# Transposing attention scores by half rows of TensorE, two at a time, in an attention and two-layer MLP kernel

## The chip, the core and the metric

The kernel runs on one core of one Trainium2 chip. The core has TensorE for matmuls (PE in the profile; its weight loads are listed apart as PEld), VectorE (DVE), ScalarE (ACT), GpSimd (POOL) and SyncE (SP), which issues most of the DMAs. The metric is the time of one execution on the device in microseconds (us), the median of a few runs.

## What is computed

Three stages follow one another. All arrays are float32.

```python
batch, n_heads, seq, head_dim = (2, 12, 448, 64)
scores = np.matmul(q, k.transpose(0, 1, 3, 2)) / np.sqrt(64)   # causal mask above the diagonal
attn = np.exp(scores - max) / (sum + 1e-9)
out = np.matmul(attn, v)                       # heads side by side: x, 896 tokens x 768
h = x @ w_in;  g = h * np.clip(h + 3, 0, 6) / 6;  x = g @ w_out     # 768 -> 2048 -> 768
h = x @ w_in2; g = P(h) / (Q(h) + 1e-6);          y = g @ w_out2    # P cubic, Q in |h| and h*h
```

## The kernel before

**Attention.** The heads are worked on two at a time: 12 pairs, each of one batch and two heads. The 448 query rows of a head are cut into seven strips of 64 rows, r = 0 to 6, and strip r looks at (r + 1) * 64 keys. The strip r of both heads lies in one tile of 128 partitions, one head on each half; these are the tiles e_91 to e_97 (r = 0 to 6) for even pairs and e_98 to e_104 for odd pairs. The steps of a pair n are:

- `scores`: 14 matmuls, each on a quarter of TensorE (64 rows by 64 columns), into four PSUM banks;
- `max` on DVE, seven instructions: masked scores go to the e tiles, with the maximum of each row (the profile's CUSTOM_DVE_ANT_0, L457, and a short read of the accumulator);
- `exp` on ACT, seven, each with the sum of its rows; `bias` and `reciprocal` of the sums, once for the strips 6, 5, 0 ("straight") and once for 4, 3, 2, 1 ("swapped");
- `norm`: the e tiles times the reciprocals, on POOL (L488) for the pairs 1 to 9, and on POOL, DVE or ACT for the others;
- `transpose` (L494): the e tiles are cut into 16 blocks of 128 rows by 128 keys, in four groups (`GROUPS`) of four, each group into one bank;
- `move` (L497 f., a copy on DVE or ACT): one bank of 512 columns to SBUF, four times a pair;
- `apply` (L514): 16 matmuls of the transposed blocks with v, on the two column halves of TensorE, into one bank o;
- `x hi` on ACT and `x rest` on DVE (L526, writes xl): o is split into two float32r parts.

**Products.** Each matrix product is made of three TensorE passes of 448 columns (high by high, low by high, high by low parts; xh, xl and so on in the profile). Weights come in chunks of three tiles. A chunk goes through `w load` (a DMA into raw), `top` (ACT), `join` (DVE, L641, writes full), `w hi` (ACT or POOL) and `w rest` (DVE or POOL, L659). All 2304 matmuls of the products stand at L729. The sums of the products may hold all eight PSUM banks, and no product may start before the last pair's scores (`scored`).

**What sets the order.** Nothing is written down in program order. `Program.order` is a list scheduler that runs when the kernel is built: each step has a cost for each engine that may do it, a due time (the pair's own time `t`, 5.5 apart, plus `DUE` of its kind and, for some pairs, `SHIFT`), and the tiles that it reads, writes and allocates. It picks the step that can begin first (within `LOOK`) and, among equals, that which is due first; `STAY` is added to the due time of a step that would put TensorE into another tiling (`TILING`). `banks` limits how many PSUM banks each use holds: scores 4, transposes 2 ("t"), o 1, out of eight. On the chip each engine then works through its own queue in that order, waiting on semaphores.

Of the kernel before, what the change touches and what calls it, by code (L numbers as in the profile page):

```python
# [8 lines left out]
F32 = mybir.dt.float32  # L9
# [10 lines left out]
P = 128  # L20
CP = 64
# [19 lines left out]
class Program:  # L41
# [13 lines left out]
    }  # L55
    BANKS = 8

    TILING = {"scores": "quarters", "apply": "columns"}
    DRAIN = 0.16
    STAY = 22.65  # L60
    LOOK = {"pe": 0.244, "dve": 0.000, "act": 0.000, "pool": 0.830, "dma": 0.000}
    UNTIL = 90.0

    def __init__(self, rings, banks, due):
# [3 lines left out]
    def add(self, kind, at, engines, fn, *args, reads=(), writes=(), new=()):  # L68

        self.ops.append((kind, at, engines, fn, args, tuple(reads), tuple(writes), tuple(new)))
# [124 lines left out]
def c_act(n):  # L197
    return 0.051 + n / 1200


def c_dve(n):
    return 0.068 + n / 960
# [12 lines left out]
def c_pe(n, passes):  # L215
    return passes * (0.0025 + n / 2400)
# [6 lines left out]
def c_mm(n, passes):  # L223
# [2 lines left out]


DUE = {
    "load": -169.78,
    "keep": 0.00,  # L230
    "fetch": -20.00,
    "load v": -160.42,
    "norm": -298.28,
    "scores": 315.32,
    "max": 50.63,
    "exp": 213.93,
    "bias": -18.96,
    "reciprocal": 22.57,
    "transpose": -74.01,
    "move": 210.62,  # L240
    "apply": -55.68,
    "x hi": 156.92,
    "x rest": 260.06,
    "constants": 64.75,
    "w load": -41.79,
    "top": 181.03,
    "join": 339.16,
    "w hi": 262.44,
    "w rest": 56.54,
    "product": 0.00,  # L250
    "relu": -117.34,
    "gate": 172.42,
    "g hi": -99.35,
    "g rest": 280.77,
    "y hi": 20.80,
    "y rest": 12.60,
    "affine": 7.80,
# [13 lines left out]
    "store": 7.50,  # L271
}
PAIR = 5.5
SHIFT = {0: -20.39, 1: -6.41, 2: -0.83, 10: 17.95, 11: 31.46}


def plan(KM, KF):
# [17 lines left out]
def tile_attention_moe_moe2(  # L295
# [24 lines left out]
    def skew(pool, size):  # L320
# [7 lines left out]
    EB, VB = 2, 3  # L328
    rings = {
        "raw": 5, "full": 3, "top": TOPS, "w": 4,  # L330
        "qr": 4, "kr": 4, "v": 3, "stat": 3, "et": 6,
        "p": 4, "qy": 3,
    }
    rings.update({f"e{r}": EB for r in range(NCH)})
    prog = Program(rings, {"s": 4, "t": 2, "o": 1, "sum": 8}, DUE)
    add = prog.add
    bank = [psum.tile([P, 512], F32, name=f"bank{n}") for n in range(prog.BANKS)]

# [3 lines left out]
    def copy(e, out, in_):  # L342
        if e is nc.scalar:
            e.activation(out, in_, AF.Copy)  # L344
        else:
            e.tensor_copy(out, in_)


    def x_tiles(nm):
# [8 lines left out]
    at = attn.enter_context(tc.tile_pool(name="at", bufs=2))  # L358
    tiles = {}

    ident = at.tile([P, P], F32, name="ident", bufs=1)
# [4 lines left out]
    halves = [slice(j * D, (j + 1) * D) for j in range(2)]  # L366
    blocks = [r // 2 + 1 for r in range(NCH)]
    es = [
        [at.tile([P, P * blocks[r]], F32, name=f"e{r}{x}", bufs=1) for r in range(NCH)]
        for x in range(EB)  # L370
    ]
    vs = [at.tile([P, KB, 2 * D], F32, name=f"v{x}", bufs=1) for x in range(VB)]
# [26 lines left out]
    for x in range(EB):  # L399
# [3 lines left out]
        new=[("o", "warm")],  # L403
# [10 lines left out]
    def v_load(e, n):  # L414
# [7 lines left out]
    SCORES = 0, 2, 6, 4, 5, 1, 3  # L422
    BANKS = ((6, 0), (4, 2), (5,), (3, 1))
    GROUPS = [
# [4 lines left out]
    ]  # L429
    APPLY = [[0, 1, 2, 3]]  # L430

    def slots(r):
        return (0, 1) if r in STRAIGHT else (1, 0)
# [54 lines left out]
            e.tensor_scalar(t, t, by, 1.0, ALU.mult, ALU.mult)  # L488

    def a_transpose(e, n, g, banks):  # L490
        pt = tiles["pt", n, g] = bank[banks[0]]
        to = pt.rearrange("p (s b q) -> p b s q", s=2, q=CP)
        for x, (r, c) in enumerate(GROUPS[g]):
            e.transpose(to[:, x], es[n % EB][r][:, c * P:(c + 1) * P], ident)  # L494

    def a_move(e, n, g):
        et = tiles["et", n, g] = at.tile([P, 512], F32, tag="et", name=f"et{n}_{g}", bufs=rings["et"])  # L497
        copy(e, et, tiles.pop(("pt", n, g)))

    def a_apply(e, n, a, banks=None):  # L500
        if a == 0:
            tiles["o", n] = bank[banks[0]]
        o, vt = tiles["o", n], vs[n % VB]
        for g in APPLY[a]:
            et = tiles.pop(("et", n, g)).rearrange("p (s b q) -> p s (b q)", s=2, q=CP)
            runs = []
            for x, (r, c) in enumerate(GROUPS[g]):
                if runs and runs[-1][2] == c and runs[-1][1] + runs[-1][3] == r:
                    runs[-1][3] += 1
                else:  # L510
                    runs.append([x, r, c, 1])
            for m, (x, r, c, count) in enumerate(runs):
                for j, slot in enumerate(slots(r)):
                    e.matmul(  # L514
                        o[halves[j], r * CP:(r + count) * CP], vt[:, c, halves[j]],
                        et[:, slot, x * CP:(x + count) * CP], start=g == 0 and m == 0,
                        stop=g == len(GROUPS) - 1 and m == len(runs) - 1,
                    )

# [11 lines left out]
    for n in range(len(pairs)):  # L531
        t, last = PAIR * n + SHIFT.get(n, 0.0), n == len(pairs) - 1
        for which in ("kr", "qr"):
            raw = which, n
            add(
                "load", t, {"act" if n == 0 and which == "qr" else "dma": 1.26}, qk_load, which, n,
                writes=[raw], new=[(which, raw)],
            )
        add(
            "load v", t, {"dma": 0.9}, v_load, n, reads=[("empty", n % VB)], writes=[("v", n), ("turn", "v")],  # L540
            new=[("v", ("v", n))],
        )
        sc = [("sc", n, held) for held in BANKS]
        add(
            "scores", t, {"pe": 1.42}, a_scores, n, reads=[("kr", n), ("qr", n)],
            writes=sc + ["scored"] * last, new=[("s", key) for key in sc],
        )
        for late, r in enumerate(order):
            w, first, mine = (r + 1) * CP, late == 0, next(held for held in BANKS if r in held)
            add(  # L550
                "max", t + late, {"dve": c_dve(w)}, a_max, n, r,
                reads=[("sc", n, mine), "masks"] + [("stat", n)] * (not first)
                + [("m", n, mine[0])] * (r != mine[0]),
                writes=[("e", n, r), ("st", n, r), ("m", n, r), ("turn", r)] + [("stat", n)] * first,
                new=[(f"e{r}", ("e", n, r))] + [("stat", ("stat", n))] * first,
            )
            add(
                "exp", t + late, {"act": 0.235 + c_act(w)}, a_exp, n, r, reads=[("stat", n)],
                writes=[("e", n, r), ("st", n, r)],
            )  # L560
        for part, held in enumerate((STRAIGHT, SWAPPED)):
            add(
                "bias", t + 2 * part, {"act": 0.2, "dve": 0.1}, a_bias, n, part,
                reads=[("st", n, r) for r in held] + [("stat", n)], writes=[("r", n, part)],
            )
            add(
                "reciprocal", t + 2 * part, {"dve": 0.15}, a_recip, n, part, reads=[("stat", n)],
                writes=[("r", n, part)],
            )
            for r in held:  # L570
                w = (r + 1) * CP
                add(
                    "norm", t + 2 * part, c_norm(n, r, w), a_norm, n, r,
                    reads=[("r", n, part), ("stat", n)], writes=[("e", n, r)],
                )
        for g, group in enumerate(GROUPS):
            add(
                "transpose", t + g, {"pe": 0.436}, a_transpose, n, g,
                reads=["masks", ("pads", n % EB)] + [("e", n, r) for r in sorted({r for r, _ in group})],
                writes=[("pt", n, g)], new=[("t", ("pt", n, g))],  # L580
            )
            add(
                "move", t + g, {"act": c_act(512), "dve": c_dve(512)}, a_move, n, g,
                reads=[("pt", n, g)], writes=[("et", n, g)], new=[("et", ("et", n, g))],
            )
        for a, gs_ in enumerate(APPLY):
            cols = 1024 * len(gs_) // len(GROUPS)
            add(
                "apply", t + 2 * a, {"pe": c_pe(cols, 4) + 0.08}, a_apply, n, a,
                reads=[("et", n, g) for g in gs_] + [("v", n)], writes=[("o", n)],  # L590
                new=[("o", ("o", n))] if a == 0 else (),
            )
        b, hp = pairs[n]
        add("x hi", t, {"act": c_act(S)}, a_hi, n, reads=[("o", n)], writes=[("x", hp, b)])
        add("x rest", t, {"dve": c_dve(S)}, a_lo, n, reads=[("o", n)], writes=[("x", hp, b)])
# [372 lines left out]
```

## Time and profile before

| | before |
|---|---|
| median of 3 runs | 547.02 us (546.81 to 547.05) |
| the profiled execution | 547.23 us |
| its span, first to last instruction | 545.4 us |
| PE busy | 535.4 us (98%) |
| PEld busy | 491.7 us (90%) |
| DVE busy | 363.0 us (67%) |
| ACT busy | 342.5 us (63%) |
| POOL busy | 37.5 us (7%) |

The first matmul begins 2.07 us into the span; attention takes the first 82 us, products the rest. PE's busy time is the union of its instructions, whose ends are modelled, so being busy does not mean that the array streams at its peak.

### The profile page before, as it was taken

To read this page: it belongs to the slowest core of one execution; us is meant where nothing else is said; L and a number is where in the kernel's file an instruction comes from. 1 tells how busy PE (TensorE), PEld (TensorE's weight loads), DVE (VectorE), ACT (ScalarE), POOL (GpSimd) and SP (SyncE) were. 2 spreads that over 40 slices of the span, in tenths; PEclk is the share of its full clock that TensorE was granted. 3 is DMA by queue.
4 is the path that set the end of the run, shared out by engine and by line. 5 is a ranking of instruction groups with operands and counts; after the bars stand their busy time and mean duration, and the time that the engine had idled before them with its cause. 6 is when DMAs were issued, how large, how long until landed. Compare 5 with 4: busy or idle time off the path is not lost.

```text
span 545.4 us, 9102 instructions
## 1 busy us (share of the span) xinstructions
PE 535.4 (98%) x3236; PEld 491.7 (90%) x3236; DVE 363.0 (67%) x814; ACT 342.5 (63%) x752; POOL 37.5 (7%) x91
## 2 busy tenths in 40 slices
PE   6999999999999999999999999999999999999997
PEld 5778889999999999999999998899999999999996
DVE  3789975677877765445543189988888888853310
ACT  4899985576777665455443187776777677645210
POOL 2486500000000000000000000000000000000000
PEclk9899999999999999999999999999999999999999
DMA  6787402477877778767775321543343234236100
GB/s 165 200 250 207 139 2 88 136 240 219 268 232 264 236 248 269 269 218 241 234 282 157 107 87 59 165 124 88 96 134 119 87 100 133 88 118 205 46 34 34
DMA packets 39309, 87.07 MB, mean 160 GB/s; under 512 B 4704, under 2 KB 14688, under 8 KB 39264
## 3 DMA queue, kind: packets, MB, share of 16 engines
q1 hardware_dynamic: 39104, 86.27, 50.2%
q8 instruction: 25, 0.41, 0.3%
q10 hardware_dynamic: 160, 0.23, 0.1%
q14 instruction: 20, 0.16, 0.1%
HBM read 71.14 MB, written 15.34 MB: 159 GB/s over the span
## 4 chain that ended last, share of the span: by engine, by line
PE 92%; DVE 5%; ACT 1%; DMA 1%; issue 0%; POOL 0%; POOLq 0%; ACTq 0%; DVEq 0%
PE bank L729 79%; PE bank L494 4%; PE bank L514 4%; PE bank L445 4%; PE bank L394 1%; DVE e L457 1%; DMA w<-kept 1%; DVE qy L794 1%; DVE p L778 1%; DVE p L804 1%; DVE p L781 0%; DVE qy L802 0%; DVE rl L788 0%; DVE p L806 0%; ACT p L774 0%
## 5 line engine op out<-in xcount | busy, mean ns | idle before, releaser
L729 PE MATMUL bank<-yh,w 128*128 128x448 f32 x384 | 112.0, 362 | 1.2 <-DVE w L659 1.2
L636 ACT ACTIVATE top<-raw 128x384 f16<-128x384 bf16 x128 | 78.7, 639 | 46.1 <-DVE full L641 39.6
L659 DVE TENSOR_TENSOR w<-full,w 128x384 fp32r<-128x384 f32 x94 | 52.5, 558 | 77.0 <-ACT w L344 76.9
L344 ACT ACTIVATE w<-full 128x384 fp32r<-128x384 f32 x92 | 48.3, 525 | 82.8 <-PE bank L729 82.7
L729 PE MATMUL bank<-rh,w 128*128 128x448 f32 x384 | 97.3, 363 | 0.4 <-DMA w<-kept 0.4
L729 PE MATMUL bank<-xh,w 128*128 128x448 f32 x384 | 93.4, 363 | 0.0
L729 PE MATMUL bank<-ph,w 128*128 128x448 f32 x384 | 92.5, 362 | 0.0
L729 PEld LDWEIGHTS bank<-yh,w 128*128 128x128 f32 x384 | 71.9, 187 | 6.2 <-DVE w L659 1.6
L729 PEld LDWEIGHTS bank<-rh,w 128*128 128x128 f32 x384 | 71.8, 188 | 5.9 <-ACT qy L797 0.8
L729 PEld LDWEIGHTS bank<-ph,w 128*128 128x128 f32 x384 | 72.0, 188 | 5.0
L729 PEld LDWEIGHTS bank<-xh,w 128*128 128x128 f32 x384 | 71.7, 188 | 5.0
L641 DVE SCALAR_TENSOR_TENSOR full<-raw,top 128x384 uint32<-128x384 uint32 x128 | 69.1, 558 | 1.5
L729 PE MATMUL bank<-yl,w 128*128 128x448 f32 x192 | 69.6, 363 | 0.0
L729 PE MATMUL bank<-rl,w 128*128 128x448 f32 x192 | 54.3, 361 | 0.0
L729 PE MATMUL bank<-pl,w 128*128 128x448 f32 x192 | 53.9, 362 | 0.0
L729 PE MATMUL bank<-xl,w 128*128 128x448 f32 x192 | 53.9, 362 | 0.0
L464 ACT ACTIVATE e<-e,stat 128x448 f32<-128x448 f32 (+6 forms) x84 | 42.5, 526 | 8.0 <-DVE stat L457 8.0
L729 PEld LDWEIGHTS bank<-yl,w 128*128 128x128 f32 x192 | 36.0, 188 | 2.6
L729 PEld LDWEIGHTS bank<-rl,w 128*128 128x128 f32 x192 | 36.0, 187 | 2.5
L457 DVE CUSTOM_DVE_ANT_0 e<-bank,mask 128x256 f32<-128x256 f32 (+6 forms) x84 | 31.6, 414 | 9.9 <-PE bank L445 9.8
L729 PEld LDWEIGHTS bank<-pl,w 128*128 128x128 f32 x192 | 36.0, 187 | 2.2
L729 PEld LDWEIGHTS bank<-xl,w 128*128 128x128 f32 x192 | 36.0, 187 | 2.2
(59 smaller groups left out, 646.9 us busy)
## 6 DMA issues: line engine op xcount, KB each, us to landing
raw<-in_w SPq DMA_DIRECT2D x128, 383.8 KB, 3.6
kept<-ws SPq DMA_DIRECT2D x32, 384.0 KB, 4.6
w<-kept SPq DMA_DIRECT2D x32, 384.0 KB, 3.3
kr<-in_kT SPq DMA_DIRECT2D x24, 112.0 KB, 3.6
out_T<-o SPq DMA_DIRECT2D x12, 224.0 KB, 2.8
qr<-in_qT SPq DMA_DIRECT2D x22, 112.0 KB, 3.3
v<-in_v SPq DMA_DIRECT2D x12, 128.0 KB, 3.1
v<-in_v SPq DMA_DIRECT2D x12, 96.0 KB, 3.5
```

The lines of the kernel that those rows point to most:

```text
L344: e.activation(out, in_, AF.Copy)
L394: e.matmul(bank[banks[0]][:, :P], ident, ident, start=True, stop=True)
L445: e.matmul(tiles["sc", n, r][halves[slot]], q[halves[j], r * CP:w], k[halves[j], :w], start=True, stop=True,)
L457: e.tensor_tensor_reduce(es[n % EB][r][:, :w], tiles.pop(("sc", n, r)), mask[:, S - w:], -0.125, 3.0e38, ALU.add, ALU.min, tiles["stat", n ...
L464: e.activation(t, t, AF.Exp, bias=stat[:, 0, at_:at_ + 1], scale=-1.0, accum_out=stat[:, 1, at_:at_ + 1],)
L494: e.transpose(to[:, x], es[n % EB][r][:, c * P:(c + 1) * P], ident)
L514: e.matmul(o[halves[j], r * CP:(r + count) * CP], vt[:, c, halves[j]], et[:, slot, x * CP:(x + count) * CP], start=g == 0 and m == 0, stop ...
L636: e.activation(out, raw[i].bitcast(BF16)[:, :, :, 2], AF.Copy)
L641: e.scalar_tensor_tensor(full[i].bitcast(U32), bits, 13, top.pop(i), ALU.logical_shift_right, ALU.bitwise_or)
L659: e.tensor_tensor(split[i][:, 1], full.pop(i), split[i][:, 0], ALU.subtract)
L729: e.matmul(sums[which, m, b], split[i][:, w, j, :], x, start=k == 0 and n == 0, stop=last and n == 2,)
L778: e.tensor_tensor(p, p, h, ALU.mult)
```

## The change

A transpose handled a block of 128 rows, which are the 64 rows of a strip for each of the two heads. Now a block is transposed as two halves: the 64 rows of one head on the upper half of TensorE's rows and the 64 of the other on the lower half, each into a bank of its own, with a 64 by 64 identity as the moving operand. So there are 32 transposes a pair in place of 16, each with 64 columns in place of 128. A bank then holds one slot of eight blocks, and the four groups become two steps of eight blocks; each step allocates two banks and is followed by two moves. "t" may hold three banks. The transposes have a tiling of their own ("rows") in the scheduler's table. All due times, `SHIFT`, `STAY` and `LOOK` have new values, so that the order changes on each engine.

```diff
-    TILING = {"scores": "quarters", "apply": "columns"}
+    TILING = {"scores": "quarters", "transpose": "rows", "apply": "columns"}
...
-    STAY = 22.65
-    LOOK = {"pe": 0.244, "dve": 0.000, "act": 0.000, "pool": 0.830, "dma": 0.000}
+    STAY = 16.37
+    LOOK = {"pe": 0.278, "dve": 0.000, "act": 0.000, "pool": 0.000, "dma": 0.000}
...
-    "join": 339.16,
+    "join": 294.60,
...
-SHIFT = {0: -20.39, 1: -6.41, 2: -0.83, 10: 17.95, 11: 31.46}
+SHIFT = {0: -137.52, 1: -87.41, 2: -49.23, 10: 28.19, 11: 35.07}
...
-    prog = Program(rings, {"s": 4, "t": 2, "o": 1, "sum": 8}, DUE)
+    prog = Program(rings, {"s": 4, "t": 3, "o": 1, "sum": 8}, DUE)
...
-        [(5, 0), (6, 0), (5, 1), (6, 1)],
-        [(5, 2), (6, 2), (6, 3), (0, 0)],
-        [(1, 0), (2, 0), (3, 0), (4, 0)],
-        [(2, 1), (3, 1), (4, 1), (4, 2)],
+        [(5, 0), (6, 0), (5, 1), (6, 1), (5, 2), (6, 2), (6, 3), (0, 0)],
+        [(1, 0), (2, 0), (3, 0), (4, 0), (2, 1), (3, 1), (4, 1), (4, 2)],
...
     def a_transpose(e, n, g, banks):
-        pt = tiles["pt", n, g] = bank[banks[0]]
-        to = pt.rearrange("p (s b q) -> p b s q", s=2, q=CP)
+        pt = [bank[b] for b in banks]
...
         for x, (r, c) in enumerate(GROUPS[g]):
-            e.transpose(to[:, x], es[n % EB][r][:, c * P:(c + 1) * P], ident)
+            for slot, rows in enumerate(halves):
+                e.transpose(
+                    pt[slot][:, x * CP:(x + 1) * CP], es[n % EB][r][rows, c * P:(c + 1) * P],
+                    ident[rows, rows],
+                )
```

What follows is the order of instructions on an engine, without times. On TensorE, in the middle of attention, before: the first group of the swapped strips of an odd pair (e_99 to e_102 are its strips 1 to 4), then the second.

```order
L494 MATMUL bank_74<-ident,e_99 128x2x64
L494 MATMUL bank_74<-ident,e_100 128x2x64
L494 MATMUL bank_74<-ident,e_101 128x2x64
L494 MATMUL bank_74<-ident,e_102 128x2x64
L494 MATMUL bank_77<-ident,e_100 128x2x64
L494 MATMUL bank_77<-ident,e_101 128x2x64
L494 MATMUL bank_77<-ident,e_102 128x2x64 x2
```

The same place of the changed kernel, where an apply of the pair before stands ahead; the first half of the step is shown.

```order
L516 MATMUL bank_79<-et_1_0_958,v_105 64x64
L493 MATMUL bank_76<-ident,e_99 128x64
L493 MATMUL bank_77<-ident,e_99 128x64
L493 MATMUL bank_76<-ident,e_100 128x64
L493 MATMUL bank_77<-ident,e_100 128x64
L493 MATMUL bank_76<-ident,e_101 128x64
L493 MATMUL bank_77<-ident,e_101 128x64
L493 MATMUL bank_76<-ident,e_102 128x64
L493 MATMUL bank_77<-ident,e_102 128x64
```

Each block became two instructions, into two banks in turn. From the third pair on TensorE's queue repeats one round: scores of pair n + 2, the first step of n + 1, apply of n, the second step of n + 1.

On DVE, after the last max of a pair, up to the first max of the next, before (et is a move, xl the `x rest` step, full a join of weights, w a `w rest`, stat the small bias and reciprocal steps):

```order
L659 TENSOR_TENSOR w_691<-full_668,w_691 128x384
L641 SCALAR_TENSOR_TENSOR full_748<-raw_484,top_113 128x384
L476 TENSOR_SCALAR stat_683<-stat_683 128x3
L346 COPY et_2_764<-bank_80 128x512
L480 RECIPROCAL stat_683<-stat_683 128x3
L659 TENSOR_TENSOR w_757<-full_748,w_757 128x384
L526 TENSOR_TENSOR xl_83<-bank_78,xh_82 128x448
L457 ISA e_104,stat_811<-bank_73,mask 128x448
```

And in the changed kernel:

```order
L473 TENSOR_SCALAR stat_864<-stat_864 128x3
L346 COPY et_0_0_917<-bank_74 128x512
L477 RECIPROCAL stat_864<-stat_864 128x3
L346 COPY et_0_1_940<-bank_73 128x512
L346 COPY et_1_0_958<-bank_75 128x512
L528 TENSOR_TENSOR xl_85<-bank_79,xh_84 128x448
L454 ISA e_97,stat_967<-bank_77,mask 128x448
L454 ISA stat_967 128x1
L477 RECIPROCAL stat_864<-stat_864 128x4
```

Three of the four moves of a pair are now DVE's and one is ACT's, in each of the pairs 1 to 9, where the two engines shared them about equally; the second reciprocal stands behind the next pair's first max. The joins and splits of weights are gone from these pairs: one join stood in nearly each pair from the third on, and now the first stands behind the first max of the last pair. Ahead of the last xl there are eight joins in both kernels, and five split chunks.

On POOL, the first steps after its constants, before (stat_219 belongs to pair 1):

```order
L488 TENSOR_SCALAR e_104<-e_104,stat_219 128x448
L488 TENSOR_SCALAR e_103<-e_103,stat_219 128x384
L488 TENSOR_SCALAR e_98<-e_98,stat_219 128x64
L488 TENSOR_SCALAR e_102<-e_102,stat_219 128x320
L488 TENSOR_SCALAR e_101<-e_101,stat_219 128x256
```

And in the changed kernel (stat_201 belongs to pair 0):

```order
L485 TENSOR_SCALAR e_96<-e_96,stat_201 128x384
L485 TENSOR_SCALAR e_95<-e_95,stat_201 128x320
L485 TENSOR_SCALAR e_92<-e_92,stat_201 128x128
L485 TENSOR_SCALAR e_104<-e_104,stat_219 128x448
L485 TENSOR_SCALAR e_103<-e_103,stat_219 128x384
```

Three norms of pair 0 moved to POOL: one of the straight strips and two of the swapped ones. Before, DVE did four of that pair's norms and ACT three; now DVE does the other four and ACT none.

## Rows read from the trace of the kernel before

**Rows 1.** Waits of PE, whole span: who, for whom, total us, times, longest

```profile
PE bank L494 <- DVE e L488: 2.9, 2, 2.1
PE bank L394 <- POOL ident masks.py:199: 2.1, 1, 2.1
PE bank L729 <- DVE w L659: 1.2, 1, 1.2
```

**Rows 2.** Busy time (x instructions) by stretch, then PE clock, DMA share, GB/s

```profile
core 0: us, PE busy (x) PEld busy (x) DVE busy (x) ACT busy (x) POOL busy (x), PEclk, DMA share, GB/s
15.00:67.20 52.20, 52.19 (x690) 42.14 (x688) 46.12 (x195) 50.43 (x172) 33.98 (x69) 0.97 0.69 200
82.00:120.00 38.00, 38.00 (x196) 35.56 (x191) 24.55 (x47) 22.76 (x46) 0.00 (x0) 1.00 0.46 146
```

**Rows 3.** Timeline of PE: start us, us, what, count; a row merges like instructions

```profile
14.52 1.74 PE L494 MATMUL bank<-ident,e 128*128 128x128 f32 x8 [0.82 <-DVE e L488]
16.19 2.72 PE L445 MATMUL bank<-kr,qr 64*64 64x64 f32 x28
...
60.72 1.09 PE L494 MATMUL bank<-ident,e 128*128 128x128 f32 x8
61.75 1.74 PE L445 MATMUL bank<-kr,qr 64*64 64x64 f32 x28
63.42 1.98 PE L514 MATMUL bank<-et,v 128*64 128x128 f32 x32
65.33 1.97 PE L494 MATMUL bank<-ident,e 128*128 128x128 f32 x16
67.23 1.74 PE L445 MATMUL bank<-kr,qr 64*64 64x64 f32 x28
...
82.07 0.68 PE L729 MATMUL bank<-xh,w 128*128 128x448 f32 x2
```

**Rows 4.** Timeline of PEld: first and second load of 65.33, first eight of 61.74

```profile
65.33 0.14 PEld L494 LDWEIGHTS bank<-ident,e 128*128 128x128 f32 x1
65.39 0.14 PEld L494 LDWEIGHTS bank<-ident,e 128*128 128x128 f32 x1
61.74 0.21 PEld L445 LDWEIGHTS bank<-kr,qr 64*64 64x64 f32 x8 [0.17 <-issue]
```

**Rows 5.** Timeline of DVE in pairs 7 and 8: start us, us, what

```profile
51.02 0.61 DVE L526 TENSOR_TENSOR xl<-bank,xh 128x448 fp32r<-128x448 f32 x1
51.55 0.77 DVE L641 SCALAR_TENSOR_TENSOR full<-raw,top 128x384 uint32<-128x384 uint32 x1
52.25 0.61 DVE L457 CUSTOM_DVE_ANT_0 e<-bank,mask 128x448 f32<-128x448 f32 x1
52.79 0.08 DVE L457 DVE_READ_ACCUMULATOR2_ANT stat<- 128x1 f32 x1
...
53.00 0.69 DVE L346 COPY et<-bank 128x512 f32<-128x512 f32 x1
53.61 0.17 DVE L480 RECIPROCAL stat<-stat 128x4 f32<-128x4 f32 x1
53.70 0.19 DVE L457 CUSTOM_DVE_ANT_0 e<-bank,mask 128x64 f32<-128x64 f32 x1
...
55.37 0.17 DVE L476 TENSOR_SCALAR stat<-stat 128x3 f32<-128x3 f32 x1
55.45 0.28 DVE L457 CUSTOM_DVE_ANT_0 e<-bank,mask 128x128 f32<-128x128 f32 x1
...
55.66 0.17 DVE L480 RECIPROCAL stat<-stat 128x3 f32<-128x3 f32 x1
```

**Rows 6.** PE clock of a stretch early in attention

```profile
14.80:18.20 3.40, 3.40 (x30) 0.50 0.60 158
```

**Rows 7.** Timeline of POOL: the four swapped norms of pair 1

```profile
20.26 1.74 POOL L488 TENSOR_SCALAR e<-e,stat 128x320 f32<-128x320 f32 x4 [1.29 <-DVE stat L480]
```

**Rows 8.** Timeline of DVE: first max of pair 2 and of pair 11

```profile
18.21 0.62 DVE L457 CUSTOM_DVE_ANT_0 e<-bank,mask 128x448 f32<-128x448 f32 x1 [0.93 <-PE bank L445]
...
69.02 0.62 DVE L457 CUSTOM_DVE_ANT_0 e<-bank,mask 128x448 f32<-128x448 f32 x1
```

**Rows 9.** Timeline of ACT in pair 7: start us, us, what

```profile
47.81 0.70 ACT L464 ACTIVATE e<-e,stat 128x448 f32<-128x448 f32 x1
48.36 0.25 ACT L464 ACTIVATION_READ_ACCUMULATOR e<-e,stat 128x1 f32 x1
...
52.24 0.46 ACT L464 ACTIVATE e<-e,stat 128x128 f32<-128x128 f32 x1
...
52.62 0.70 ACT L636 ACTIVATE top<-raw 128x384 f16<-128x384 bf16 x1
```

More of the change, by code (lines that the diff above doesn't have):

```diff
@@ L228 @@
 DUE = {
-    "load": -169.78,
+    "load": -70.29,
     "keep": 0.00,
     "fetch": -20.00,
[L232 to L246, printed above, removed]
-    "join": 339.16,
-    "w hi": 262.44,
-    "w rest": 56.54,
+    "load v": -286.97,
+    "norm": -92.70,
+    "scores": 78.41,
+    "max": -7.32,
+    "exp": -40.38,
+    "bias": -181.52,
+    "reciprocal": -23.19,
+    "transpose": -255.27,
+    "move": 143.82,
+    "apply": -41.05,
+    "x hi": -23.57,
+    "x rest": -56.33,
+    "constants": -84.40,
+    "w load": 262.37,
+    "top": 237.74,
+    "join": 294.60,
+    "w hi": 177.64,
+    "w rest": 54.50,
     "product": 0.00,
[L251 to L254, printed above, removed]
+    "relu": -335.43,
+    "gate": -172.47,
+    "g hi": -125.93,
+    "g rest": 321.20,
     "y hi": 20.80,
@@ L424, in tile_attention_moe_moe2 @@
     GROUPS = [
[4 rows of a table removed]
+        [(5, 0), (6, 0), (5, 1), (6, 1), (5, 2), (6, 2), (6, 3), (0, 0)],
+        [(1, 0), (2, 0), (3, 0), (4, 0), (2, 1), (3, 1), (4, 1), (4, 2)],
     ]
-    APPLY = [[0, 1, 2, 3]]
     def slots(r):
@@ L490, in a_transpose, with a_move, a_apply @@
     def a_transpose(e, n, g, banks):
-        pt = tiles["pt", n, g] = bank[banks[0]]
-        to = pt.rearrange("p (s b q) -> p b s q", s=2, q=CP)
+        pt = [bank[b] for b in banks]
+        for slot in range(2):
+            tiles["pt", n, g, slot] = pt[slot]
         for x, (r, c) in enumerate(GROUPS[g]):
-            e.transpose(to[:, x], es[n % EB][r][:, c * P:(c + 1) * P], ident)
[L496 to L505, printed above, removed]
+            for slot, rows in enumerate(halves):
[3 more added lines that the diff above has]
+                )
+    def a_move(e, n, g, slot):
+        et = at.tile([P, 512], F32, tag="et", name=f"et{n}_{g}_{slot}", bufs=rings["et"])
+        tiles["et", n, g, slot] = et
+        copy(e, et, tiles.pop(("pt", n, g, slot)))
+    def a_apply(e, n, banks):
+        o, vt = bank[banks[0]], vs[n % VB]
+        tiles["o", n] = o
+        for g, group in enumerate(GROUPS):
+            et = [tiles.pop(("et", n, g, slot)) for slot in range(2)]
             runs = []
-            for x, (r, c) in enumerate(GROUPS[g]):
+            for x, (r, c) in enumerate(group):
                 if runs and runs[-1][2] == c and runs[-1][1] + runs[-1][3] == r:
@@ L515, in a_apply @@
                         o[halves[j], r * CP:(r + count) * CP], vt[:, c, halves[j]],
-                        et[:, slot, x * CP:(x + count) * CP], start=g == 0 and m == 0,
+                        et[slot][:, x * CP:(x + count) * CP], start=g == 0 and m == 0,
                         stop=g == len(GROUPS) - 1 and m == len(runs) - 1,
@@ L576, in tile_attention_moe_moe2 @@
         for g, group in enumerate(GROUPS):
+            pt = [("pt", n, g, slot) for slot in range(2)]
             add(
-                "transpose", t + g, {"pe": 0.436}, a_transpose, n, g,
+                "transpose", t + 2 * g, {"pe": 0.46}, a_transpose, n, g,
                 reads=["masks", ("pads", n % EB)] + [("e", n, r) for r in sorted({r for r, _ in group})],
-                writes=[("pt", n, g)], new=[("t", ("pt", n, g))],
+                writes=pt, new=[("t", key) for key in pt],
             )
[L582 to L592, printed above, removed]
+            for slot in range(2):
+                et = "et", n, g, slot
+                add(
+                    "move", t + 2 * g + slot, {"act": c_act(512), "dve": c_dve(512)}, a_move,
+                    n, g, slot, reads=[pt[slot]], writes=[et], new=[("et", et)],
+                )
+        add(
+            "apply", t, {"pe": c_pe(1024, 4) + 0.08}, a_apply, n,
+            reads=[("et", n, g, slot) for g in range(2) for slot in range(2)] + [("v", n)],
+            writes=[("o", n)], new=[("o", ("o", n))],
+        )
         b, hp = pairs[n]
```

## The prediction, made blind

> **What bounds the kernel now.** I read the waits of TensorE first, then the busy time by stretch, then the timelines. In the whole span PE waits 5.0 us for DVE and POOL before attention is under way, and 1.2 us once in the products [rows 1]. From 15 to 67.2 us it is busy 52.19 of 52.20 us and in the products 38.00 of 38.00 [rows 2]: both stages are bound by PE, and what attention saves on PE arrives at the end as long as no other engine takes over. The products begin in earnest at 82.07 us [rows 3]; their 2304 matmuls are the same afterwards. So the question is only when that row comes.
>
> A pair's work on PE is read from the distance of one row's start to the next in [rows 3]: scores 1.67 us (61.75 to 63.42), apply 1.91 (63.42 to 65.33), 16 transposes in one piece 1.90 (65.33 to 67.23), eight in a piece 1.03 (60.72 to 61.75). Eight more transposes cost 0.87, so one costs 0.109, and the change of tiling around a piece 0.16. From the scores of pair 2 (16.19) to those of pair 11 (67.23) a pair takes 51.04 / 9 = 5.67 us: 1.67 + 1.91 + 1.90 or 2 x 1.03.
>
> **What a step of eight blocks costs now.** It has 16 transposes of 64 columns. If the two row halves run side by side, a pair of them takes the time of 64 columns, half of 0.109, but not less than a load of weights needs. The trace of before has no load of 64 rows by 128 columns. The nearest: the second load of a transpose began 0.06 us after the first (65.39 after 65.33), at 128 columns; and in the scores, where four quarters of the array are in use, eight loads lie in 0.21 us, of which one alone takes some 0.14, so they began within 0.07 [rows 4]. Quarters of both row halves are among these, so the two halves do load, and stream, at once: 14 matmuls of the scores have 3584 columns in two passes, which at the transposes' rate (0.109 for 128 columns in one) would be 6.1 us one by one, and they took 1.67. I take 0.058 for a pair of half transposes: 8 x 0.058 + 0.16 = 0.62 us a step. Lower bound 8 x 0.0545 + 0.16 = 0.60; upper bound, if the loads of both halves follow one another at 0.058, 16 x 0.058 + 0.16 = 1.09. I take the lower end since the scores' rows show both halves loading together.
>
> The Trainium skill says otherwise of the load: by "TensorE: Matmul & The Clock Gate", section "LDWEIGHTS (loading the stationary operand)", its time goes by the columns and not by the rows, so that a load of few rows and 128 columns costs as much as a full one, and there are now twice as many. The 0.06 us between two full loads is shorter than that page's figure for 128 columns (some 107 ns), and its "TensorEngine Tiling (Array Packing)", section "Key Properties", lets tiles load in parallel, as the eight loads above did. By the first rule alone two steps a pair would gain nothing; the sum below does not use it, and the first rival does.
>
> PE then needs 1.67 + 1.91 + 2 x 0.62 = 4.82 us a pair, 0.85 less than 5.67. Were PE still the bound, nine pairs would give 7.7 us.
>
> **Who takes over.** In the changed order DVE does, in each of the pairs 1 to 9: seven max, two reciprocals, one bias, three moves (about two before), one xl. By starts in [rows 5]: max of 448 0.54 (52.25 to 52.79), five max 1.67 (53.70 to 55.37), max of 128 0.21 (55.45 to 55.66), a move 0.61 (53.00 to 53.61), a reciprocal 0.09, a bias 0.08, xl 0.53 (51.02 to 51.55). Sum 2.42 + 3 x 0.61 + 0.53 + 0.18 + 0.08 = 5.04 us. ACT: the seven exps, xh and two moves lie between 47.81 and 52.62 [rows 9], 4.81 us; with a move less (it is given less than DVE's 0.61) and a bias some 4.5. POOL: four norms 1.74 us [rows 7], all seven perhaps 3.3. So DVE is the longest at 5.04, PE next at 4.82. DVE has this little because the joins and splits left these pairs; eight joins still stand ahead of the last xl, all of them in the tail.
>
> DVE waits too: it must have scores for its next first max, which stand on PE behind the second step, which waits for the swapped norms, which wait for the reciprocal behind the max before. That round is a max 0.54, reciprocal 0.09, four norms 1.74, a step 0.62, the scores' first strips (about 1.2 of 1.67 with the hand-over), and some 0.6 for five hand-overs: about 4.8, less than 5.04, but not by much. I take 5.1 us a pair.
>
> **The front.** Pair 0's second half of transposes began at 14.52 [rows 3], when its last norms were done on DVE and ACT. Two of them are now on POOL, one after the other, at about 0.43 each [rows 7] against about 0.3 on DVE: some 0.3 later. The clock granted to PE is 0.50 from 14.80 to 18.20 [rows 6], which is the lower level, 1.2 GHz; before it PE had waited for these norms [rows 1], as it will again, so I leave it there. The eight pairs of half transposes then take some 1.2 us at that clock where 1.67 went by (14.52 to 16.19). The scores of pair 2 come at about 16.05 in place of 16.19, and the first max of pair 2 at 18.1 in place of 18.21 [rows 8]: next to nothing, though pair 0 has two steps saved, because the wait is for norms. The DMAs of v that now stand ahead of the second q cost nothing: DVE works on pair 0 until about then.
>
> **The tail.** The first max of pair 11 came at 69.02 [rows 8]; from there to 82.07 is 13.05 us. In the new order PE has four steps (2.5 us), three applies (5.7), 18 product matmuls (3.6) and the rest of the scores there, some 12.3, and DVE's last move before the last apply has seven max, four more moves, four joins, two xl and five norms ahead of it, some 10.7, to which apply and hand-overs add 2.2. I take 12.9; from 12.1 to 13.4.
>
> **The sum.** First max of pair 11: 18.1 + 9 x 5.1 = 64.0 (before 69.02, so 5.0 less); start of the products 64.0 + 12.9 = 76.9 (82.07, so 5.2 less). In the products DVE is busy 24.55 of 38 us after 82 [rows 2], and the number of joined and split chunks at the last xl is the same, so I add no wait there. The profiled execution took 547.23, 0.21 over the median: 547.2 - 5.2 = 542.0, and a median of **541.8 us**. Bounds: 5.04 a pair and the shortest tail give 540.3; 5.3 a pair and the longest tail 544.1.
>
> **Rivals.**
>
> *The halves share one path for their weights* (the other side; the page's rule, as above). Then a step is 1.09 us and a pair 1.67 + 1.91 + 2.18 = 5.76 against 5.67; ten pairs cost 0.9 us more, and with two steps where one piece of 16 stood: about 548.0. It decides from 1.03 us a step (what eight full transposes cost) upward. For it: each transpose of before has a load of its own, and there are twice as many. Against it: the eight loads of [rows 4]. Were a load 0.109, it would be 20 us. Chance 0.08.
>
> *A wait in DVE's round.* In the first pairs xl stands ahead of the third move and needs xh, which needs apply; and the round worked out above is near 5.04. If each pair loses 0.3 on top, 5.4 a pair: 18.1 + 48.6 + 13.2 = 79.9, that is 545.0. For it: DVE idled 52.20 - 46.12 = 6.1 us in nine pairs before, and ACT's records fill 50.43 of 52.20 [rows 2]. Against it: it then waited for a full PE. Chance 0.15.
>
> *The weights come late.* Eight joins in the tail in place of one after another: if the second or third chunk is late by 1 to 2 us, 543.5. For it: two POOL splits of about 1 us each stand before the third chunk. Against: it is needed only some 4 us after the last apply. Chance 0.07.
>
> *PE stays the bound*, DVE's work being shorter than I think, or the clock staying up at 14.8: 7 us and more, about 539.8. Chance 0.06.
>
> *It does nothing*, since PE was not the bound: excluded nearly by 52.19 of 52.20; 0.02.
>
> **Chances.** The forecast has 0.62 and a range of its own from 540.3 to 544.1. Three runs lie within 0.24 us; about 0.2% (1.1 us) is what I would call a difference here. Below 545.9: the forecast, the second, third and fourth rival, 0.90, less a part for what I do not see: faster 0.84; within 0.2%: 0.09; slower 0.07. The range from 540.0 to 545.2 takes in the bounds of the sum and the wait in DVE's round, and leaves out the first and the last rival and the half of the one with the full PE.
>
> **What would show it.** Right: the step of 16 half transposes takes some 0.6 us from start to start, DVE is busy nearly without a gap between the first max of pair 3 and that of pair 10, 5.0 to 5.2 us apart, PE shows waits for moves or scores' banks in that stretch, and the products are full from about 77 us on. Wrong: a step of 1.0 us or more; a first max of pair 2 away from 18 us; first maxes 5.4 us or more apart; or a PE that waits for weights after 77 us.

## The result, and the profile of the changed kernel

The changed kernel takes 541.36 us (median of four runs, 540.91 to 542.47) against 547.02; the ratio is 0.990 with a 95% interval of 0.988 to 0.992. The profiled execution took 541.22 us, 6.01 less than the one before.

Waits of PE over the whole span of the changed kernel:

```profile
PE bank L493 <- POOL e L485: 4.1, 4, 2.2
PE bank L394 <- POOL ident masks.py:199: 2.1, 1, 2.1
PE bank L732 <- DVE w L662: 1.2, 1, 1.2
```

Against [rows 1] the wait for norms has moved from DVE to POOL and grown by 1.2 us. One more wait of before, in the products, is gone:

```profile
PE bank L729 <- DMA w<-kept: 0.4, 1, 0.4
```

It is not put down to the change: it is 0.2 us in the first experiment below and 0.8 in the second.

Busy time by stretch, with the columns of [rows 2]; the second and third rows are two pieces of the front:

```profile
15.00:62.50 47.50, 47.10 (x840) 37.57 (x837) 44.82 (x193) 41.81 (x154) 28.99 (x63) 0.94 0.56 161
...
13.80:17.20 3.40, 2.70 (x32) 2.25 (x36) 2.89 (x10) 2.70 (x11) 2.14 (x5) 0.50 0.43 113
17.20:20.60 3.40, 3.40 (x40) 2.42 (x34) 2.49 (x14) 2.14 (x7) 1.73 (x4) 0.50 0.67 187
...
45.00:60.00 15.00, 15.00 (x286) 11.98 (x282) 15.00 (x69) 13.77 (x52) 9.66 (x21) 1.00 0.37 100
```

From 45 to 60 us DVE is busy all the time, which it was not in any long stretch before; its idle time from 15 to 62.5 is 2.7 us, all of it ahead of 35 us. PE reads as busy all the time too, so that busy shares alone do not say which of the two is the bound; a run below does. The granted clock is 0.50, the level of 1.2 GHz, for 6.8 us at the front, twice as long as in [rows 6]. That is a matter of the execution: in the run with the lighter apply, below, whose front is the same up to the first apply (its waits there are 2.21 and 1.55 us), it was 0.50 for half of that:

```profile
14.30:17.70 3.40, 2.96 (x36) 2.39 (x40) 2.63 (x10) 2.44 (x10) 1.88 (x5) 0.50 0.43 123
17.75:21.15 3.40, 3.00 (x64) 2.03 (x60) 3.34 (x19) 2.67 (x11) 1.73 (x4) 1.00 0.66 181
```

Timeline of PE, the columns of [rows 3]: the front, one pair, and the start of the products:

```profile
12.24 0.72 PE L493 MATMUL bank<-ident,e 64*128 64x64 f32 x16 [2.20 <-POOL e L485]
14.50 1.12 PE L493 MATMUL bank<-ident,e 64*128 64x64 f32 x16 [1.54 <-POOL e L485]
15.55 3.26 PE L442 MATMUL bank<-kr,qr 64*64 64x64 f32 x28
18.74 1.12 PE L493 MATMUL bank<-ident,e 64*128 64x64 f32 x16
...
24.41 0.72 PE L493 MATMUL bank<-ident,e 64*128 64x64 f32 x16
25.06 1.98 PE L516 MATMUL bank<-et,v 128*64 128x128 f32 x32
26.97 0.71 PE L493 MATMUL bank<-ident,e 64*128 64x64 f32 x16
27.61 1.74 PE L442 MATMUL bank<-kr,qr 64*64 64x64 f32 x28
29.29 0.71 PE L493 MATMUL bank<-ident,e 64*128 64x64 f32 x16
...
76.71 0.67 PE L732 MATMUL bank<-xh,w 128*128 128x448 f32 x2
```

A step of 16 half transposes takes 0.65 us from start to start (24.41 to 25.06), where eight full ones took 1.03 [rows 3]; a pair's work on PE is 4.88 us (24.41 to 29.29). At half clock a step is 1.05 (14.50 to 15.55) and the scores of pair 2 take 3.19 (15.55 to 18.74) instead of 1.68 (27.61 to 29.29).

Timeline of DVE in pair 7, from its first max to that of pair 8 (the moves are L346):

```profile
44.45 0.62 DVE L454 CUSTOM_DVE_ANT_0 e<-bank,mask 128x448 f32<-128x448 f32 x1
...
47.00 0.68 DVE L346 COPY et<-bank 128x512 f32<-128x512 f32 x1
47.60 0.17 DVE L477 RECIPROCAL stat<-stat 128x3 f32<-128x3 f32 x1
47.68 1.26 DVE L346 COPY et<-bank 128x512 f32<-128x512 f32 x2
48.86 0.62 DVE L528 TENSOR_TENSOR xl<-bank,xh 128x448 fp32r<-128x448 f32 x1
49.39 0.62 DVE L454 CUSTOM_DVE_ANT_0 e<-bank,mask 128x448 f32<-128x448 f32 x1
```

No row has a wait: a pair is 4.94 us of DVE's own work. The first maxes of the pairs 6 to 11 come at 39.52, 44.45, 49.39, 54.32, 59.25 and 64.18, all 4.93 or 4.94 apart.

The products begin at 76.71 us, 5.36 earlier than in [rows 3], and from there to the end of the span it is 462.7 us in place of 463.3. The two make up the 6.0 us. Of the 5.36, 0.5 cannot be put down to the change: the first max of pair 0 came at 8.04 us and in the kernel before at 8.54, and in the runs below it lies anywhere between 7.29 and 8.64.

```profile
8.54 0.62 DVE L457 CUSTOM_DVE_ANT_0 e<-bank,mask 128x448 f32<-128x448 f32 x1 [8.54 <-PE bank L445]
...
8.04 0.62 DVE L454 CUSTOM_DVE_ANT_0 e<-bank,mask 128x448 f32<-128x448 f32 x1 [8.04 <-PE bank L442]
```

### The profile page after: what moved, and what is told of

Read it like the earlier page. It is cut to its first block, busy times and chain, and to the rows that moved or that the text cites. A ratio compares the mean times of both kernels' runs of the same rounds, so it can differ in the third digit from the quotient of the medians.

```text
span 539.4 us, 9500 instructions
## 1 busy us (share of the span) xinstructions
PE 528.5 (98%) x3428; PEld 485.9 (90%) x3428; DVE 364.8 (68%) x818; ACT 338.9 (63%) x740; POOL 41.2 (8%) x99
## 4 chain that ended last, share of the span: by engine, by line
PE 91%; DVE 5%; ACT 1%; POOL 1%; DMA 1%; issue 1%; SPq 0%; POOLq 0%; ACTq 0%; DVEq 0%
PE bank L732 81%; PE bank L516 3%; PE bank L442 3%; PE bank L493 3%; PE bank L394 1%; DMA raw<-in_w 1%; DVE e L454 1%; POOL e L485 1%; DVE qy L797 1%; DVE p L781 1%; DVE p L807 1%; DVE p L784 1%; DVE qy L805 0%; ACT e L461 0%; DVE rl L791 0%
## 5 line engine op out<-in xcount | busy, mean ns | idle before, releaser
L639 ACT ACTIVATE top<-raw 128x384 f16<-128x384 bf16 x128 | 79.9, 640 | 58.2 <-DVE full L644 44.9
```

The source lines that it names most:

```text
L639: e.activation(out, raw[i].bitcast(BF16)[:, :, :, 2], AF.Copy)
```

## The experiments

Each was timed beside the kernel before, which came out at medians of 546.90 to 547.23 us; a difference of some tenths between two runs that were taken at different times is therefore not clear of the noise. "First max" is DVE's first max of a pair.

**One half at a time.** The order of the 16 transposes alone:

```diff
-        for x, (r, c) in enumerate(GROUPS[g]):
-            for slot, rows in enumerate(halves):
+        for slot, rows in enumerate(halves):
+            for x, (r, c) in enumerate(GROUPS[g]):
```

> The changed kernel with the 16 half transposes of a step in another order: the eight of the upper rows first, then the eight of the lower rows, so that no two neighbours lie on different halves. Work and instruction count are the same. Theory (two half transposes load and stream side by side, which is what makes a step 0.65 us): without a partner a step takes about 1.0 to 1.1 us, TensorE needs 4.87 + 2 x 0.4 = about 5.7 us a pair and is the bound again, VectorE waits for it; about nine pairs x 0.8 = +7 us over the changed kernel, 546 to 550 us. Rival (the gain comes from smaller loads of 64 rows, not from the pairing): a step stays at 0.65 us and the time at 541 us.

547.32 us, ratio 1.0006 (0.9996 to 1.0015): the whole gain is gone. Its PE timeline:

```profile
42.53 1.01 PE L493 MATMUL bank<-ident,e 64*128 64x64 f32 x16
43.48 1.98 PE L516 MATMUL bank<-et,v 128*64 128x128 f32 x32
45.39 1.02 PE L493 MATMUL bank<-ident,e 64*128 64x64 f32 x16
46.33 1.74 PE L442 MATMUL bank<-kr,qr 64*64 64x64 f32 x28
```

A step is 0.95 us (42.53 to 43.48) for the same instructions, and first maxes are 5.48 us apart, which is PE's 1.67 + 1.91 + 2 x 0.95. So neighbours on different halves run side by side, and it is their pairing that makes 0.65; not the smaller load. The single starts in the two traces show it: in the changed kernel the partners of a pair start some 0.003 us apart and the next pair 0.062 later; here neighbours on one half also start 0.062 apart. (A step of 0.95 is less than sixteen of these, since three transposes of the second half start beside the last of the first.) The order also decides whether neighbours write into one bank or two, and that was not varied by itself; but the full transposes of before start 0.107 to 0.111 us apart whether the bank changes between them or not, so a change of bank alone lets none run side by side there.

**Due times alone, and transposes alone.** The kernel before with `DUE`, `SHIFT`, `STAY` and `LOOK` of the changed one, and the other way round.

> The kernel before with the due times, shifts, stay and look-ahead of the changed one, and nothing else. Theory (the steps are the gain): TensorE still needs its four steps a pair and stays the bound at 5.6 to 5.8 us a pair; 545 to 549 us. Rival (the due times are the gain): 543.5 us or less.

> The changed kernel with the due times, shifts, stay and look-ahead of the one before, and nothing else. Theory: most of the gain, 541.5 to 544 us, with VectorE without gaps in the middle pairs and some of the gain lost in the first and last pairs, where the shifts act. Rival (the new transposes need the new due times): 545 us or more.

The due times alone: 551.19 us, ratio 1.0074 (1.0061 to 1.0088), so 4 us slower. The transposes alone: 546.89 us, ratio 1.000 (0.999 to 1.001), nothing. Both came out beyond the range that the theory gave, the second where it matters: the rival of that run, that the new transposes need the new due times, holds. Neither half of the change gains, only both together do.

Why the transposes alone gain nothing: two stretches of the kernel before, and then the same two of that kernel (order PE, PEld, DVE, ACT, POOL):

```profile
30.00:45.00 15.00, 15.00 (x204) 12.39 (x200) 14.10 (x63) 15.00 (x53) 11.55 (x24) 1.00 0.81 235
45.00:60.00 15.00, 15.00 (x215) 12.13 (x214) 14.43 (x62) 15.00 (x51) 10.10 (x21) 1.00 0.71 209
...
30.00:45.00 15.00, 13.97 (x258) 11.11 (x252) 11.18 (x56) 15.00 (x53) 9.69 (x21) 1.00 0.81 235
45.00:60.00 15.00, 13.71 (x236) 10.86 (x238) 12.53 (x57) 15.00 (x51) 9.78 (x19) 1.00 0.44 125
```

PE is no longer full, but ACT is, and it was just as full before. The scheduler gave it 34 of the 48 moves (before 26): from 30 to 60 us it had 13 moves and six conversions of weights before, and 16 and three in this kernel. These are its groups of moves there, before and in this kernel,

```profile
L344 ACT ACTIVATE et<-bank 128x512 f32<-128x512 f32 x13 | 7.3, 624 | 0.0
...
L344 ACT ACTIVATE et<-bank 128x512 f32<-128x512 f32 x16 | 8.4, 609 | 0.0
```

and these are the groups of ACT and of DVE in the changed kernel, in the same stretch:

```profile
L344 ACT ACTIVATE et<-bank 128x512 f32<-128x512 f32 x6 | 3.5, 578 | 0.0
L346 DVE COPY et<-bank 128x512 f32<-128x512 f32 x18 | 11.7, 677 | 0.0
```

These runs point to two limits at about the same height in the kernel before. With PE made lighter and ACT left full it takes 546.89 us; with ACT relieved (13.34 and 12.26 us of 15 in these stretches) and PE at 5.48 a pair, the run with one half at a time, 547.32; with both relieved 541.36. Which of the two held the kernel before by itself is not shown: no run made ACT alone lighter under the old order.

The due times alone leave PE with two steps of 1.03 in a pair, and add waits for norms (5.0 us in five waits on POOL). From pair 2 to 11 a pair takes 6.07 us (first maxes from 17.12 to 71.71; before 5.65 [rows 8]). Two rounds, of 8.42 and 8.34 us, are the worst; in the second PE had three steps, an apply and a wait between two scores:

```profile
33.54 1.74 PE L445 MATMUL bank<-kr,qr 64*64 64x64 f32 x28
35.22 1.09 PE L494 MATMUL bank<-ident,e 128*128 128x128 f32 x8
37.04 1.09 PE L494 MATMUL bank<-ident,e 128*128 128x128 f32 x8 [0.73 <-POOL e L488]
38.06 1.98 PE L514 MATMUL bank<-et,v 128*64 128x128 f32 x32
39.97 1.09 PE L494 MATMUL bank<-ident,e 128*128 128x128 f32 x8
40.99 1.74 PE L445 MATMUL bank<-kr,qr 64*64 64x64 f32 x28
```

**Which due times.** Five of them say when weights are loaded and prepared (`w load`, `top`, `join`, `w hi`, `w rest`); four of the others are of the products (`relu`, `gate`, `g hi`, `g rest`), the rest of attention. One kernel is the changed one with the five old:

```diff
-    "w load": 262.37,
-    "top": 237.74,
-    "join": 294.60,
-    "w hi": 177.64,
-    "w rest": 54.50,
+    "w load": -41.79,
+    "top": 181.03,
+    "join": 339.16,
+    "w hi": 262.44,
+    "w rest": 56.54,
```

and one is the transposes alone with the five new; all else in it (the other due times, `SHIFT`, `STAY` and `LOOK`) is old.

> The changed kernel with five of the old due times, those of the weights (load, top, join, hi, rest), so that conversions, joins and splits of weights are dealt into the pairs again; the attention's due times stay new, and VectorE still gets 34 of the 48 moves, ScalarE 14. Theory (the deal of the moves is what the new due times are needed for): 541 to 543.5 us, at most the weights' 1 to 2 us worse. Rival (it is the weights' work in the pairs that costs): 545 us or more.

> The transposes alone (e3, all due times old), with the five due times of the weights new: their work leaves the pairs, but ScalarE still gets 32 of the 48 moves (34 in e3), VectorE 16. Theory (the deal of the moves): ScalarE stays busy nearly without a gap at 5.2 us a pair or more and the time is 544.5 to 547 us. Rival (the weights' work in the pairs): 541 to 543 us.

541.90 us, ratio 0.9906 (0.9892 to 0.9920), and 544.80 us, 0.9963 (0.9949 to 0.9977), both as the theory had it. With the attention's due times old, ACT is full also without the weights' work, and the first maxes from pair 7 on are 5.3 us apart:

```profile
45.00:60.00 15.00, 14.38 (x256) 11.55 (x256) 11.97 (x60) 15.00 (x52) 9.30 (x20) 1.00 0.30 80
```

The price is paid in a roundabout way: the last apply ends at 76.40 us, no later than in the changed kernel, since the front is quicker (pair 2's first max at 14.75); but no product stands ahead of it, where the changed kernel has 18 between 67.44 and 74.80, 3.6 us of work at 0.2 each. So what is not of the weights is worth 2.9 us (544.80 less 541.90). It lies in attention: with these 18 counted, the products take the same in both kernels. The weights' due times are worth about 2 in the one setting (546.89 less 544.80), and in the other (541.90 less 541.36) nothing that is clear of the noise. How the 2.9 splits between the deal of the moves and the rest was not tried.

**Lighter apply.** `if c: continue` ahead of apply's matmuls leaves out all keys but the first 128.

> The changed kernel with most of attention times v left out: in every pair apply multiplies only the first 128 keys (448 of 1024 columns of each half), so TensorE has about 1 us less a pair (4.87 to some 3.8 us); all other engines have what they had. Theory (VectorE is the bound of the changed kernel's attention, at 4.93 us a pair): first maxes stay 4.93 us apart, TensorE idles about 1 us a pair, and the time is 539.5 to 541.5 us, the last microsecond from the tail and the front. Rival (TensorE, at 4.87 us a pair nearly as full, is what is waited for): about 4.2 us a pair or less and 535 us or less.

541.09 us, ratio 0.989 (0.9877 to 0.9904): a microsecond less on PE in each pair changes nothing. PE's timeline:

```profile
44.09 0.71 PE L493 MATMUL bank<-ident,e 64*128 64x64 f32 x16
44.73 0.99 PE L518 MATMUL bank<-et,v 128*64 128x128 f32 x12
46.70 0.71 PE L493 MATMUL bank<-ident,e 64*128 64x64 f32 x16 [0.98 <-POOL e L485]
47.34 1.74 PE L442 MATMUL bank<-kr,qr 64*64 64x64 f32 x28
```

What was taken away came back as a wait of 0.98 for norms on POOL, which in turn waits for DVE (4.1 us in five waits from 40 to 60 us) and for PE (3.6 in four); first maxes stayed 4.93 apart (44.03 to 48.96).

**xl twice.** The counterpart, on DVE:

```diff
-        e.tensor_tensor(
-            xs[b][1][:, hp, :], tiles.pop(("o", n))[:, :S], xs[b][0][:, hp, :], ALU.subtract
-        )
+        o = tiles.pop(("o", n))[:, :S]
+        for _ in range(2):
+            e.tensor_tensor(xs[b][1][:, hp, :], o, xs[b][0][:, hp, :], ALU.subtract)
```

> The changed kernel with VectorE's subtraction of each pair's rest (xl, 0.53 us from start to start) written twice, the second time with the same result; the order of everything else is the same. Theory (VectorE is the bound in the pairs, without slack): the first maxes of the middle pairs come 5.4 to 5.5 us apart in place of 4.93, and the time is 5 to 6 us longer, 546 to 547.5 us. Rival (it has slack, and TensorE or ScalarE set the pace): 544 us or less.

547.88 us, ratio 1.0013 (1.0004 to 1.0022), 6.5 over the changed kernel and a little above the range. In DVE's timeline two xl take 1.19 us where one took 0.53:

```profile
51.04 1.27 DVE L530 TENSOR_TENSOR xl<-bank,xh 128x448 fp32r<-128x448 f32 x2
52.23 0.61 DVE L454 CUSTOM_DVE_ANT_0 e<-bank,mask 128x448 f32<-128x448 f32 x1
```

and first maxes are 5.59 apart (46.64 to 52.23): 4.93 and the 0.66 in full. DVE has no slack there, where PE could lose a microsecond a pair without effect.

**Filled norm waits.** 9 and 6 identity matmuls ahead of pair 0's two steps:

```diff
+    FILL = {(0, 0): 9, (0, 1): 6}
...
+        for _ in range(FILL.get((n, g), 0)):
+            e.matmul(pt[0][:, :P], ident, ident, start=True, stop=True)
         for x, (r, c) in enumerate(GROUPS[g]):
```

> The changed kernel with 9 matmuls of the identity ahead of the first step of transposes and 6 ahead of the second (0.21 us each, into a bank that the step overwrites), which fill the 2.20 and 1.54 us in which TensorE waits for norms there. Nothing else is changed. Theory (TensorE's clock is half from 13.8 to 20.6 us because of the idle time ahead of it, and what runs at half clock there is on the path): the granted clock stays 1.00, the scores of pair 2 take 1.7 instead of 3.3 us, and the first max of pair 3 comes 1.5 to 2.3 us earlier than at 23.98 us: 538.8 to 540.2 us. Rival 1 (the norms and VectorE set the pace at the front, not the clock): same within 0.5 us of 541.3. Rival 2 (the fillers delay the steps, or the clock falls later instead): 541 us or more.

541.65 us, ratio 0.9901 (0.9886 to 0.9917): no gain, though in the profiled execution the clock did what was expected,

```profile
13.80:20.60 6.80, 6.80 (x129) 5.62 (x131) 6.71 (x28) 5.86 (x24) 4.30 (x9) 1.00 0.65 179
```

and from the first max of pair 0 to that of pair 3 it took 13.72 us (7.29 to 21.01) in place of 15.94 (8.04 to 23.98). (In two of the five executions the mean clock was 0.997 even so, and they are the slowest, 542.24 and 543.48.) The 2.2 us were lost in the next pair, on ACT:

```profile
21.05 0.20 ACT L471 ACTIVATE stat<-stat 128x4 f32<-128x4 f32 x1
24.25 0.65 ACT L643 ACTIVATE top<-raw 128x384 f16<-128x384 bf16 x1 [3.00 <-DMA raw<-in_w]
24.77 0.64 ACT L461 ACTIVATE e<-e,stat 128x448 f32<-128x448 f32 x1
```

ACT stands at a conversion of weights that nobody needs before the tail, and behind it stand pair 3's exps, for which DVE waits: its next first max comes 7.92 us later.

**That conversion later, with and without the fillers.** After the order is made, the first two `top` are moved back in it: the first to the place of the second, the second as far behind its own.

```diff
-        return [(ops[n], where[n], given[n]) for _, _, n in sorted(result)]
+        line = [n for _, _, n in sorted(result)]
+        tops = [n for n in line if ops[n][0] == "top"][:2]
+        at = [line.index(n) for n in tops]
+        step = at[1] - at[0]
+        for n, x in zip(tops[::-1], at[::-1]):
+            line.remove(n)
+            line.insert(x + step, n)
+        return [(ops[n], where[n], given[n]) for n in line]
```

> The kernel with the filled norm waits (e5), with the first two conversions of weights (top) moved later by one pair in ScalarE's order, each to some 20 instructions behind its place; no work is added. In e5 ScalarE stood at the first of them for 3.00 us, until 24.25 us, for the weights' transfer, and the exps of pair 3 stood behind it. Theory (the clock at the front was on the path, and its gain was given back at this wait): pair 4's first max comes at about 26 instead of 28.93 us, all later ones 2.5 to 3 us earlier than in e5, and the time is 538 to 539.5 us. Rival (transfers set the pace: the loads of q, k and v are late next, or the products wait for weights): 540.5 us or more.

> The changed kernel with only the second edit of e7: the first two conversions of weights moved later by one pair in ScalarE's order, and no matmuls added. Theory (what e7 gains is the clock at the front, which the conversions gave back in e5): the granted clock falls to 0.50 at the front as in the changed kernel, the gap of 5.67 us ahead of pair 5's first max shrinks to about 5.0, and the time is 540.3 to 541.3 us. Rival (the conversions' place alone is the gain of e7): 539 us or less.

Both edits: 538.54 us, ratio 0.9843 (0.9830 to 0.9856). The conversions alone: 540.27 us, 0.9880 (0.9866 to 0.9893), where the clock falls again (0.50 from 13.8 to 17.2 us, 0.63 on average from there to 20.6). So the fillers save nothing by themselves, the later conversions 1.1 us (541.36 less 540.27; the two intervals overlap), and both 2.8. With both, DVE has no idle time from early on:

```profile
15.00:30.00 15.00, 15.00 (x288) 12.19 (x284) 15.00 (x64) 13.86 (x51) 10.12 (x22) 1.00 0.74 207
45.00:60.00 15.00, 15.00 (x288) 12.05 (x284) 15.00 (x65) 13.87 (x51) 9.83 (x22) 1.00 0.36 99
```

The first maxes of pairs 2 to 11 run from 16.03 to 60.46, 4.92 to 4.97 apart. This version is faster than both kernels.

## Why the prediction was right, step by step

| step | forecast | measured |
|---|---|---|
| a step of 16 half transposes | 0.62 us | 0.65 |
| a pair on PE | 4.82 | 4.88 |
| a pair on DVE, the bound | 5.04, taken as 5.1 | 4.93 |
| first max of pair 2 | 18.1 | 17.56 |
| first max of pair 11 | 64.0 | 64.18 |
| the tail | 12.9 | 12.53 |
| start of the products | 76.9 | 76.71 |
| profiled execution | 542.0 | 541.22 |
| median | 541.8 | 541.36 |

- *What bounds the kernel before* was read from PE's busy time, and half of it was missed. ACT was as full (15.00 of 15.00 us in both stretches above), and lighter steps under the old order saved nothing. The condition "as long as no other engine takes over" was thus not met under that order, and the rival that it does nothing, set at 0.02 on PE's busy share, is what came of the transposes alone. The forecast held since the new order also takes moves off ACT, whose load it counted (some 4.5 us a pair) for the new order only.
- *The step* was priced from loads that overlap, and the run with one half at a time shows that they must: 0.95 without a partner. The rival in which the halves share one path, 1.03 us or more a step, is out. The rule behind it, in the Trainium skill's "TensorE: Matmul & The Clock Gate", section "LDWEIGHTS (loading the stationary operand)", that a load costs by its columns whatever its rows, gives 107 ns for 128 columns and thus, by an estimate from that figure, 1.7 us for 16 loads one after the other. The step took 0.65, and even neighbours on one half started 0.062 us apart, so here the measurement decides. The same page of the Trainium skill, in the section "The mechanism", lets loads for other row groups overlap with running matmuls, and the two orders of one step, 0.65 and 0.95, agree with that.
- *Who takes over* was the right question and the right engine. Only the experiments show it, for PE too reads as full: a microsecond off PE changed nothing, 0.66 on DVE came through whole. The rival with PE still the bound is out. But the sign that was named for it, waits of PE for moves or scores' banks, did not come: with 4.88 us of a pair's 4.93, PE shows no wait from 45 to 60 us.
- *DVE's pair* was 0.1 too long: three moves took 1.78 us and not 1.83, the seven max 2.39 and not 2.42, and the allowance of 0.06 for its round was not used; the rival of a wait in that round is out for the middle pairs.
- *The front* has an error that the sum hides. Pair 2's first max is right by the distance from pair 0's: 9.52 us (8.04 to 17.56), and 9.56 by the forecast (8.54 to 18.1). I left the half clock as it was; in this execution it lasted twice as long, and pair 3's first max came at 23.98, not at 18.1 + 5.1 = 23.2. Pair 5's, at 34.59 against 33.4, was later still: a conversion of weights stood on ACT ahead of exps (with it moved, that gap fell from 5.67 us to 5.16), of the kind of my third rival but at the front and not in the tail. From pair 2's first max to pair 5's it was 1.7 us more than forecast. Six pairs of 4.93 in place of 5.1 gave 1.0 us of it back and the early start 0.5: that pair 11's came within 0.2 us is luck to that extent.
- *The tail* and the rest of the span were 0.4 and 0.6 us shorter than I took them, the last in part since the wait of 0.4 us for kept weights was not there in this execution.
- *The range.* Its lower end, from 5.04 a pair and the shortest tail, is 540.5 by its own terms and not 540.3; nothing hangs on it.
- *The change was not taken apart.* The sum credited the gain to PE's shorter steps and read DVE's load off the new order as a given. That the new order is half of the change, without which ACT stays full and nothing is gained, was in none of the rivals; two runs showed it.

## What to carry to other kernels

When a step on the bounding engine gets cheaper, add up the next engines' work under the order that will really run: here the same cheaper transposes were worth nothing under one order, in which ACT got most of the moves and stayed full, and 5.7 us under another. Look at every engine's busy time before naming one the bound; two engines that both read as full are told apart by making each lighter or heavier by itself. And time won at the front arrives only if nothing that waits for a transfer stands in an in-order queue ahead of urgent work; move such an instruction back before judging the gain.

## What the runs showed of the hardware

- Two transposes of 64 rows on different row halves went at the pace of one: partners started some 0.003 us apart and pairs 0.062, where neighbours on one half started 0.062 apart and full ones 0.109. A step of 16 took 0.65 us in alternation and 0.95 with all of one half ahead of the other.
- The granted clock fell to 0.50, the level of 1.2 GHz, after PE had stood for 2.20 and 1.54 us, with 0.7 us of transposes between. How long it stayed there differs between executions: 6.8 us in the changed kernel's profile, 3.4 in that with the lighter apply after the same waits. In the profiled executions it stayed at 1.00 with matmuls of the identity in those gaps, and also with the old due times and the new transposes, after a single wait of 2.08 us there.
- With the transposes alone the time follows the mean clock of the execution: 546.1 to 546.4 us in the four executions at 0.999 or 1.000, 547.7 to 548.3 in the five at 0.992 to 0.994. The four executions of the changed kernel show no such order.
- The first max of pair 0 came between 7.29 and 8.64 us in the profiled executions; why was not looked into. That spread is as large as several of the differences that were looked for, so starts are best compared as distances from this first max.
